# A gated mix of a long state-space convolution and a top-2 expert on one core: the hand-ordered kernel rewritten as one list-scheduled graph

## Chip, cores, metric

One core of one Trainium2 chip. The metric is the device time of one execution in microseconds (us), lower is better; the time before is the median of three runs.

## The reference, cut to what matters

```python
x = A_u                                            # 1 x 2048 x 512, bf16
g = sigmoid((x * gate_w).sum(-1))                  # one gate a token
# a: per channel d a kernel K[d, l] of 2048 lags from 128 complex modes n
dt = exp(log_dt); P = exp((dt * A)[:, :, None] * l)         # l in bf16
K  = einsum("dn,dnl,dn->dl", C, P, dt * B).real
a  = irfft(rfft(pad(x)) * rfft(pad(K)))[:2048] + x * Dskip  # along the tokens
# b: the two tokens with the largest r = x @ w_r go through an expert
y  = (silu(x_sel @ w_gate) * (x_sel @ w_up)) @ w_down * sigmoid(r_sel)
b  = x + scatter_add(0, idx, y)
out = g * a + (1 - g) * b
```

Rounding lags to bf16 leaves 2048 lags with few distinct values. Each distinct value is written as a sum of a lag t1 (table T1) and a lag t2 (table T2), so a tap is a product of two table rows summed over the 128 modes.

## The kernel before, in words

Everything runs on 128 partitions in bf16, with fp32 sums in PSUM. Helper functions record the operations: every vector tensor_tensor has line 306 (`TT`), tensor_scalar lines 309 and 310 (`TS`), copies 314 (`CP`), and every activation line 316 (`ACTV`). `Sched` (lines 46 to 117) keeps each engine's operations in the order in which the program names them and puts a wait in front of an operation for each buffer that it reads or writes, its own engine's last writer of that buffer included (lines 66 to 72). The order of the whole program is thus the order of the source, written by hand at lines 851 to 880.

- **Loads** (320 to 338): six parameter matrices, log_dt, the input u, gate vectors, expert matrices W_gate and W_up, and one 5.4 MB block of transform matrices, all issued at the start on SP's queue.
- **Parameters** (340 to 381): transposes on PE, then some twenty vector operations of 128x512 fp32.
- **Tables** (`lag_group`, 395 to 444, driven by `kgen_tables`, 629 to 658): for each half of 256 channels 32 lags of T1 and 21 of T2 in groups of four. Each lag has an exponential of its own (416), two phase arguments as int32 (403 on ScalarE or 406 on VectorE), and each group one sine over the low 16 bits; then products of magnitude and cosine or sine on VectorE, for T2 eight products and sums a group, since the weights C·B·dt are multiplied in.
- **Routing and expert** (`routing_and_moe`, 454 to 624): a generator of which one or two steps run between the table groups of the first half.
- **Taps** (`kgen_mm`, 659 to 678): per half 256 pairs of matmuls of 32x24 outputs, one pair a channel, with `tile_position`; 16-byte and 512-byte steps in their operands. 1024 matmuls in all stand at lines 670 and 674. `post` (679 to 714) gathers the taps of a chunk of 128 channels (690) and turns them into spectra of four blocks of 512 lags (707).
- **Convolution** by overlapped blocks of 512 for four chunks of 128 channels: `forward` (726, matmuls at 739), `products` (747, VectorE), `xu_inv` (770: (1-g)·x plus the expert row at 778 and 779, the inverse at 789, each evicted to SBUF by itself), and `mix_a`, `mix_p`, `mix_o` (830 to 842: skip term, gate, sum, store). The last chunk is done in four pieces (`final_fine`, 796).

Of the kernel before, what the change touches and what calls it, by code (L numbers as in the profile page):

```python
# [26 lines left out]

class Buf:

    def __init__(self, name, parents=()):  # L30
        self.name = name
        self.last_w = None
        self.readers = []
        self.parents = list(parents)

    def prior(self):
        out = []
        for p in self.parents:
            if p.last_w is not None:
                out.append(p.last_w)  # L40
            out.extend(p.readers)
            out.extend(p.prior())
        return out


class Sched:
    def __init__(self, nc, block_sems):
        self.nc = nc
        self.ops = {e: [] for e in ENGS}
        self.sem = dict(block_sems)  # L50
        self.cnt = {e: 0 for e in ENGS}
        self.known = {e: {} for e in ENGS}
        self.dma_sems = []
        self.dma_free = []
        self.final_waits = []

    def _deps(self, eng, reads, writes):
        deps = {}
        def add(ev):
            if ev is None:  # L60
                return
            s, v = ev
            k = id(s)
            if self.known[eng].get(k, 0) >= v:
                return
            if k not in deps or deps[k][1] < v:
                deps[k] = (s, v)
        for b in reads:
            add(b.last_w)
        for b in writes:  # L70
            add(b.last_w)
            for r in b.readers:
                add(r)
            for r in b.prior():
                add(r)
        out = list(deps.values())
        for s, v in out:
            self.known[eng][id(s)] = v
        return out

    def _commit(self, ev, reads, writes):
        for b in reads:
            b.readers.append(ev)
        for b in writes:
            b.last_w = ev
            b.readers = []

    def op(self, eng, fn, reads=(), writes=()):
        waits = self._deps(eng, reads, writes)
# [4 lines left out]
        return ev

    def dma(self, fn, sem, n=1, reads=(), writes=(), eng=SP, final=False):
        waits = self._deps(eng, reads, writes)
        ev = (sem, 16 * n)
        self.ops[eng].append((fn, waits, (sem, 16)))
        self._commit(ev, reads, writes)  # L100
        if final:
            self.final_waits.append(ev)
        return ev

    def emit(self, eng, h):
        for fn, waits, inc in self.ops[eng]:
# [54 lines left out]
def kspec_mats(L=2048):
    lq = bf16_lag(np.arange(L))
    rep = {}
    for j, t2 in enumerate(LQ_T2):
        for k, t1 in enumerate(LQ_T1):
            q = t1 + t2
            if q not in rep:
                rep[q] = (j, k)  # L170
    th = theta()
    out = np.zeros((len(KUSE), 128, 2 * BLK))
    cover = np.zeros(L, dtype=bool)
    for u, (i, jg) in enumerate(KUSE):
# [750 lines left out]
```

## Time and profile before

| what | value |
|---|---|
| runs | 374.71, 376.3, 377.43 us; median 376.3 |
| span of the profiled execution | 373.4 us (its first to its last instruction) |
| the same execution's own time | not listed apart from the three runs, which lie 1.3 to 4.0 us above the span |
| VectorE (DVE) busy | 270.7 us, 72% |
| ScalarE (ACT) busy | 239.4 us, 64% |
| TensorE (PE) busy | 188.9 us, 51%; mean granted clock 0.696 of full |
| HBM read, written | 14.27 MB, 2.10 MB |

Busy is the time in which an engine works on an instruction. Each row of an instruction view names line, engine, operation, output and input with their shapes, the count, busy time in us and the mean ns of one, and behind the last bar the idle time in front with what ended it. In the view of one source line the three numbers are the shortest, median and longest duration in ns, and then come the first and the last start. RT, RK, RS, RU and RC are the five SBUF arenas, ps is PSUM.

### The profile page before, as it was taken

The numbers are of one execution on the slowest core, as the hardware profiler recorded it, in microseconds if no ns is written. First come the engines' busy times: TensorE is split into PE (matmuls) and PEld (weight loads), VectorE is DVE, ScalarE is ACT, GpSimd is POOL, SyncE is SP. The second block draws the span as 40 slices with busy tenths as digits, with TensorE's granted clock in tenths as the row PEclk, the third lists the DMA queues.
The fourth block names the chain that finished last, engine by engine and source line by source line (L and its number), as shares of the span: only waits on it lengthen the run. The fifth ranks groups of instructions, "written<-read, shape, count | busy, mean of one in ns | idle before, by whom it ended". The sixth has DMA issues, their size and how long they took to land.

```text
span 373.4 us, 8503 instructions
## 1 busy us (share of the span) xinstructions
PE 188.9 (51%) x3674; PEld 170.3 (46%) x3674; DVE 270.7 (72%) x495; ACT 239.4 (64%) x385; POOL 1.7 (0%) x6
## 2 busy tenths in 40 slices
PE   2600301432300076704343803889899999998810
PEld 2500300330100076704343703789889889886810
DVE  0795658562599992878105999999999299899555
ACT  2899453399596999566999981553753484481461
POOL 0000010000000000000000000000000000000000
PEclk9855555555655556855856865689989969969785
DMA  6999000005000000000000000000000000200222
GB/s 154 275 443 438 26 3 0 0 11 187 0 1 0 0 4 5 2 1 2 1 2 0 2 0 2 4 4 4 2 2 2 3 2 2 58 3 2 58 67 45
DMA packets 18261, 16.91 MB, mean 45 GB/s; under 512 B 12848, under 2 KB 17072, under 8 KB 18096
## 3 DMA queue, kind: packets, MB, share of 16 engines
q1 hardware_dynamic: 18224, 16.37, 13.3%
q8 instruction: 29, 0.48, 0.5%
q14 instruction: 8, 0.07, 0.1%
HBM read 14.27 MB, written 2.10 MB: 44 GB/s over the span
## 4 chain that ended last, share of the span: by engine, by line
ACT 36%; DVE 32%; PE 26%; issue 4%; DMA 1%; SPq 1%; ACTq 0%; DVEq 0%
DVE RT L306 23%; ACT RT L316 21%; PE ps L739 10%; ACT RK L316 8%; PE ps L789 5%; DVE RT L310 5%; ACT L316 3%; PE ps L707 2%; ACT RT L837 2%; PE ps L670 2%; PE ps L674 1%; PE ps L779 1%; PE ps L778 1%; PE ps L607 1%; DVE RT L309 1%
## 5 line engine op out<-in xcount | busy, mean ns | idle before, releaser
L306 DVE TENSOR_TENSOR RT<-RT 128x1024 bf16<-128x1024 bf16 (+5 forms) x146 | 101.2, 704 | 29.7 <-ACT RT L316 19.3
L316 ACT ACTIVATE RT<-ps 128x512 bf16<-128x512 f32 (+3 forms) x79 | 51.8, 662 | 55.4 <-PE ps L739 22.8
L739 PE MATMUL ps<-RU,RC 128*128 128x128 bf16 x896 | 55.7, 228 | 16.7 <-ACT RK L316 16.6
L310 DVE TENSOR_SCALAR RT<-RS 128x256 int32<-128x256 f32 x148 | 49.2, 341 | 19.1 <-ACT RT L403 14.9
L739 PEld LDWEIGHTS ps<-RU,RC 128*128 128x128 bf16 x896 | 54.8, 103 | 17.1 <-issue 16.9
L306 DVE TENSOR_TENSOR RT<-RT,RK 128x4096 bf16<-128x4096 bf16 (+3 forms) x32 | 55.0, 1761 | 8.5 <-ACT RT L316 8.4
L316 ACT ACTIVATE RT<-RT 128x2048 bf16<-128x2048 int16 (+1 forms) x28 | 50.3, 1811 | 9.8 <-DVE RT L310 9.8
L670 PE MATMUL ps<-RT 128*32 128x24 bf16 x512 | 22.7, 286 | 52.1 <-DVE RT L306 52.1
L670 PEld LDWEIGHTS ps<-RT 128*32 128x32 bf16 x512 | 21.2, 171 | 52.9 <-DVE RT L306 52.4
L316 ACT ACTIVATE RT<-RS 128x256 bf16<-128x256 f32 x74 | 30.8, 416 | 3.5 <-DVE RS L306 1.2
L707 PE MATMUL ps<-RS,RC 128*128 128x128 bf16 x288 | 20.4, 240 | 20.2 <-ACT RS L316 17.6
L707 PEld LDWEIGHTS ps<-RS,RC 128*128 128x128 bf16 x288 | 19.5, 110 | 21.0 <-ACT RS L316 18.2
L316 ACT ACTIVATE RK<-ps 128x512 bf16<-128x512 f32 x32 | 19.1, 595 | 15.3 <-PE ps L707 5.9
L306 DVE TENSOR_TENSOR RT<-RT,RS 128x1024 bf16<-128x1024 bf16 (+1 forms) x48 | 27.8, 619 | 0.4
L789 PE MATMUL ps<-RT,RC 128*128 128x128 bf16 x384 | 27.7, 247 | 0.0
L403 ACT ACTIVATE RT<-RS 128x256 int32<-128x256 f32 x64 | 26.4, 416 | 1.9
L789 PEld LDWEIGHTS ps<-RT,RC 128*128 128x128 bf16 x384 | 27.2, 113 | 0.3
L837 ACT ACTIVATE RT<-RT,RS 128x128 bf16<-128x128 bf16 x48 | 19.2, 401 | 12.5 <-DVE RT L306 11.0
L674 PE MATMUL ps<-RT 128*32 128x24 bf16 x512 | 22.9, 286 | 3.8 <-issue 3.8
L674 PEld LDWEIGHTS ps<-RT 128*32 128x32 bf16 x512 | 21.8, 169 | 4.1 <-issue 4.1
L306 DVE TENSOR_TENSOR RT<-RK,RT 128x1024 bf16<-128x1024 bf16 x16 | 11.1, 691 | 13.2 <-ACT RT L316 12.9
L316 ACT ACTIVATE RK<-RS 128x256 bf16<-128x256 f32 x32 | 19.4, 605 | 1.0
(66 smaller groups left out, 189.8 us busy)
## 6 DMA issues: line engine op xcount, KB each, us to landing
RC<-c_mats SPq DMA_DIRECT2D x1, 5376.0 KB, 24.5
RU<-in_A_u_dram SPq DMA_DIRECT2D x4, 512.0 KB, 8.0
RK<-in_B_w_gate_dram SPq DMA_DIRECT2D x1, 1792.0 KB, 9.4
RK<-in_B_w_up_dram SPq DMA_DIRECT2D x1, 1792.0 KB, 13.4
RK<-in_B_w_down_dram SPq DMA_DIRECT2D x1, 1792.0 KB, 7.5
out_dram<-RT SPq DMA_DIRECT2D x3, 512.0 KB, 3.8
out_dram<-RT SPq DMA_DIRECT2D x4, 128.0 KB, 2.0
RT<-in_A_A_re_dram SPq DMA_DIRECT2D x1, 128.0 KB, 2.6
```

The source lines that it names most:

```text
L306: return S.op(eng, lambda h: h.tensor_tensor(out=o, in0=a_, in1=b_, op=op), reads=rd, writes=wr)
L309: return S.op(eng, lambda h: h.tensor_scalar(out=o, in0=a_, scalar1=s1, scalar2=None, op0=op0), reads=rd, writes=wr)
L310: return S.op(eng, lambda h: h.tensor_scalar(out=o, in0=a_, scalar1=s1, scalar2=s2, op0=op0, op1=op1), reads=rd, writes=wr)
L316: return S.op(ACT, lambda h: h.activation(out=o, in_=a_, func=func, scale=scale), reads=rd, writes=wr)
L403: S.op(ACT, lambda h, i=i, t=t, cs=cs: h.activation(out=ARG(0, 128, ((gi * 2 + cs) * 4 + i) * HC, (1, HC)), in_=B16(0, 128, c0, (1, HC)), ...
L607: last = h.matmul(P32(by_, 0, 2, 0, (1, D)), HB(0, 128, 6 * 28 + fb * 2, (1, 2)), WD(0, 128, fb * D, (1, D)), start=(fb == 0), stop=(fb == ...
L670: h.matmul(P32(b, 32 * c4, 32, cq * 24, (1, 24)), TP(0, 128, (ch // 8) * 512 + (ch % 8), (8, 32)), TQ(0, 128, ch, (HC, 24)), start=True, s ...
L674: last = h.matmul(P32(b, 32 * c4, 32, cq * 24, (1, 24)), TP(0, 128, (ch // 8) * 512 + 256 + (ch % 8), (8, 32)), TQ(0, 128, NSLOT * HC + ch ...
L707: last = h.matmul(P32(bb[hb_], 0, 128, tl * 128, (1, 128)), CM(0, 128, OF_KP + u * 1024 + tau * 128, (1, 128)), KC(0, 128, kb * 768 + KUSE ...
L739: last = h.matmul(P32(bb[hb_], 0, 128, tl * 128, (1, 128)), CM(0, 128, of + tc * 1024 + tau * 128, (1, 128)), U(0, 128, tb * D + ck * 128, ...
L789: last = h.matmul(P32(b, 0, 128, tt * 128, (1, 128)), CM(0, 128, OF_G + sc * 512 + tt * 128, (1, 128)), YHs[vb](0, 128, j * 1024 + sc * 12 ...
L837: S.op(ACT, lambda h, tb=tb, vb=vb: h.activation(out=YA(0, 128, vb * 2048 + tb * 128, (1, 128)), in_=YA(0, 128, vb * 2048 + tb * 128, (1, ...
```

## The change

A new class `Graph` takes every operation with the engines that may run it and a duration for each, a rank from a table of names, and its buffers. `schedule` walks through a simulated time: a free engine takes the ready operation of the highest rank for which SBUF and PSUM have room, and then SBUF addresses are packed. `link` puts in waits, leaving out those that an earlier wait already implies, and PE's waits for itself. The order of each engine is thus fixed before the program runs.

```diff
+RANKS = [("ld pnA", 990), ... ("exp z", 800), ("polar0", 790), ("exp t1_0", 640), ("sin0", 650),
+ ("X0", 646), ("X1", 635), ("A1_0", 600), ..., ("tap 0", 590), ("Kh 0", 580), ("sin1", 515), ("A1_1", 500),
+ ("spread", 495), ("tap 1", 490), ("Kh 1", 480), ("gather", 470), ("ffn", 470), ("Y0.0", 420), ("inv 0", 400),
+ ("ld inv", 400), ("ld w", 390), ("Y1.0", 320), ("inv 1", 300), ...]
+for o in avail[e]:                                  # schedule(): the choice of a free engine
+    if o.ready > t or (best is not None and o.prio <= best.prio): continue
+    if o.pref and e != o.pref and free[o.pref] < t + o.opts[e][1]: continue
```

The tables. Eight lags of T2 and its steps are made from exponential and sine (`DIRECT`), for 512 channels at once; the other lags are complex products of table rows (`cmul`, four products and two sums, four lags of 256 channels each), and the weights come in with the first product, for half h A1, A2, B, C, D:

```diff
+DIRECT = [129, 130, 131, 132, 4, 256, 512, 1024]
+for i, t in enumerate(DIRECT):
+    e1.append(g.op("exp z%d" % t, {ACT: (... ca(512))}, ...))
...
+    for cs in range(2):
+        g.op("arg z%d.%d" % (t, cs), {DVE: (... cd(512))}, [br], [ba[cs]])
+    for hh_ in range(2):
+        s1.append(g.op("sin z%d.%d" % (t, hh_), {ACT: (... ca(512))}, ba, [bZ[hh_][i]], after=e1))
+for hh_ in range(2):
+    for i0, n in ((0, 4), (4, 1), (5, 3)):
+        g.op("polar%d z%d" % (hh_, i0), {DVE: (pol, cd(512 * n))}, ...)
...
+for i, (pa, pb) in enumerate(((0, 0), (1, 1), (0, 1), (1, 0))):
+    g.op("%s.m%d" % (name, i), {DVE: (... op=ALU.mult), cd(n))}, ...)
+for part in range(2):
+    g.op("%s.a%d" % (name, part), {DVE: (... op=(ALU.subtract if part == 0 else ALU.add)), cd(n))}, ...)
```

(The last four lines are in `cmul`; n is 1024.) T1 has the lags 8·m for m from -16 to 15 (`T1K`). Sine and cosine are made for m = 1 to 16 and serve both signs; the products at the end are of 128x2048, two of them in each half of 128x1792:

```diff
+for m in [m for mm in range(1, 17) for m in (mm, -mm) if m != 16]:
+    e2.append(g.op("exp t1_%d %d" % (h, m), {ACT: (... out=tT1[h](BF, 0, 128, s * 4, (128, NG), (1, 4)), ... ca(256))}, ...))
...
+for q in range(8):
+    for cs in range(2):
+        for i in range(2):
+            g.op("arg%d %d.%d" % (h, m, cs), {DVE: (... cd(256)), ACT: (... ca(256))}, [br], [ba[2 * cs + i]], pref=DVE)
+    for cs in range(2):
+        sins.append(g.op("sin%d %d.%d" % (h, q, cs), {ACT: (... ca(512))}, ..., after=e2))
...
+for ck in range(2):
+    tt("t1_%d t1i+.%d" % (h, ck), ...); tt("t1_%d t1r+.%d" % (h, ck), ...)
+    g.op("neg sin %d.%d" % (h, ck), {DVE: ..., ACT: ...}, [], sq + [bsn[ck]], pref=DVE)
+    tt("t1_%d t1i-.%d" % (h, ck), ...); tt("t1_%d t1r-.%d" % (h, ck), ...)
```

The sines wait for all exponentials of their half (`after=e2`), and the exponentials of half 1 for the sines of half 0 (`after=after_e`). The forward transform is one of 1024 tokens for two blocks, 512 channels wide, folded by even and odd tokens; the taps take four channels a matmul:

```diff
+for j in range(eo, 8, 2):
+    r = h.matmul(o, tF(BF, 0, 128, ((j * 2 + ri) * 4 + ft) * 128, (1, 128)), tU(BF, 0, 128, (b * 8 + j) * D, (1, D)), ...)
+if b == 1:
+    r = h.matmul(o, ident() if plus else nident(), eov(0, 1 - ri, row, (1, D)), start=False, stop=True)
...
+tt("spread %d.%d.%d" % (b, ri, sd), ..., cd(2048))
...
+hh.matmul(o, tT1[h](BF, 0, 128, gr * 128, (1, 128)), tT2[h](BF, 0, 128, 4 * gr, (HC, NSL), (1, 4)), start=True, stop=False)
+r = hh.matmul(o, tTI[h](BF, 0, 128, gr * 128, (1, 128)), tT2[h](BF, 0, 128, NSL * HC + 4 * gr, (HC, NSL), (1, 4)), ...)
+TAP1 = g.ops[-1:]
...
+g.dma("ld wg", ..., 1835e3, writes=[bWG], after=TAP1, bias=-30)
+g.dma("ld wu", ..., 1835e3, writes=[bWU], after=TAP1, bias=-30)
+g.dma("ld inv%d" % b, ..., 1048e3, writes=[bG[b]], after=TAP1, bias=-10)
+g.dma("ld wd", ..., 1835e3, writes=[bWD], after=TAP1, bias=-30)
+g.dma("ld U2_%d" % b, ..., 1048e3, writes=[bU2[b]], after=TAP1)
```

That makes 32 rows of X with 4 matmuls (block 0) or 5 (block 1) of 512 columns, 8 `spread`, 64 groups of two tap matmuls of 84 columns a half, then a half 88 small matmuls `sel` and 104 `Kh` of 256 columns; what PE writes is evicted 1024 elements at a time. TAP1 is the last tap of half 1. W_down goes into W_gate's tile (`tWD = tWG`), so its load also waits for the first expert matmuls.

The spectra of K stay in SBUF as whole tiles of a half. The products are 40 operations of 128x2048 and 8 folds; the inverse adds (1-g)/g times x, the expert row and the convolution in PSUM, and the gate is the scale of its eviction, two of 128x256 for each of 16 `inv` (the skip term is the tap of lag 0: Dskip is a row of the spectrum's operand, `ld dskip`):

```diff
+o = ps(F32, 0, 128, (2 * hb + jj) * 256, (1, 256))
+hh.matmul(o, tDG(...), tU2[blk](...), start=True, stop=False)
+hh.matmul(o, tOR(BF, 0, 2, ...), tZB(BF, 0, 2, 1024 + h * HC, (1, HC)), start=False, stop=False)
+for ft in range(4):
+    for ri in range(2):
+        r = hh.matmul(o, tG(...), tS(...), start=False, stop=(ft == 3 and ri == 1))
...
+g.op("inv %d.%d.%d" % (h, blk, 2 * q + hb), {PE: (iv_, 0.109 * 20)}, bS + [bG[q], bDG, bOR[blk], bZB[2], bU2[blk]], ...)
+r = hh.activation(..., in_=ps(F32, 0, 128, i * 256, (1, 256)), func=ACTF.Copy, scale=g32(0, 128, blk * 8 + 4 * q + i, (1, 1)))
...
-        def xu_inv(ck): ...
-        def mix_a(ck): ...
-        def mix_p(ck): ...
-        def mix_o(ck): ...
```

## Rows read from the trace of the kernel before

**Rows 1.** Page, part 1: busy us, share of the span and instructions of each engine.
```profile
PE 188.9 (51%) x3674; PEld 170.3 (46%) x3674; DVE 270.7 (72%) x495; ACT 239.4 (64%) x385; POOL 1.7 (0%) x6
```

**Rows 2.** Page, part 4: the chain that ended last, shares by engine.
```profile
ACT 36%; DVE 32%; PE 26%; issue 4%; DMA 1%; SPq 1%; ACTq 0%; DVEq 0%
```

**Rows 3.** Stretches of the span: length, busy time by engine, PE clock, DMA.
```profile
52.00:101.00 49.00, 14.04 (x226) 9.11 (x226) 28.14 (x94) 29.98 (x46) 0.00 (x0) 0.53 0.11 38
...
357.00:374.00 17.00, 0.00 (x0) 0.00 (x0) 9.83 (x26) 5.10 (x10) 0.00 (x0) 0.63 0.27 62
...
250.00:326.00 76.00, 74.72 (x1187) 68.67 (x1184) 65.77 (x82) 39.34 (x75) 0.00 (x0) 0.93 0.04 9
```

**Rows 4.** Groups of DVE instructions by form.
```profile
L310 DVE TENSOR_SCALAR RT<-RS 128x256 int32<-128x256 f32 x148 | 49.2, 341 | 19.1 <-ACT RT L403 14.9
...
L306 DVE TENSOR_TENSOR RT<-RT 128x2048 bf16<-128x2048 bf16 x14 | 17.1, 1224 | 7.6 <-ACT RT L837 7.0
...
L306 DVE TENSOR_TENSOR RT<-RT 128x512 f32<-128x512 f32 x12 | 7.8, 687 | 0.2
...
L309 DVE TENSOR_SCALAR RT<-RT,RS 128x2048 bf16<-128x2048 bf16 x4 | 2.8, 748 | 4.7 <-ACT RT L316 4.7
```

**Rows 5.** DVE's instructions in order of time, merged: start us, us to the last's end.
```profile
11.34 0.43 DVE L314 CAST RT<-RS 128x512 f32<-128x512 bf16 x1 [11.34 <-ACT RS L316]
...
24.30 5.09 DVE L310 TENSOR_SCALAR RT<-RS 128x256 int32<-128x256 f32 x16
...
131.47 11.25 DVE L310 TENSOR_SCALAR RT<-RS 128x256 int32<-128x256 f32 x16
...
230.30 13.24 DVE L306 TENSOR_TENSOR RT<-RT,RK 128x4096 bf16<-128x4096 bf16 x2
...
280.00 2.35 DVE L306 TENSOR_TENSOR RT<-RT,RK 128x2048 bf16<-128x2048 bf16 x2
282.26 2.87 DVE L306 TENSOR_TENSOR RT<-RT 128x1024 bf16<-128x1024 bf16 x4
285.05 1.29 DVE L306 TENSOR_TENSOR RT<-RT,RK 128x1024 bf16<-128x1024 bf16 x2
...
324.75 4.49 DVE L306 TENSOR_TENSOR RT<-RT,RK 128x4096 bf16<-128x4096 bf16 x2 [1.62 <-ACT RT L316]
```

**Rows 6.** Groups of ACT instructions by form.
```profile
L316 ACT ACT_TABLE_LOAD x12 | 15.4, 1283 | 0.9 <-PEq L910 0.7
...
L316 ACT ACTIVATE RT<-ps 128x1024 bf16<-128x1024 bf16 x8 | 8.2, 1022 | 0.6
...
L316 ACT ACTIVATE RT<-RT 128x512 bf16<-128x512 int16 x2 | 1.2, 612 | 0.0
```

**Rows 7.** ACT's instructions in order of time, merged.
```profile
12.53 14.31 ACT L316 ACTIVATE RT<-RS 128x256 bf16<-128x256 f32 x32 [1.22 <-DVE RS L306]
...
190.92 1.27 ACT L316 ACTIVATE RK<-ps 128x512 bf16<-128x512 f32 x2
192.08 5.19 ACT L403 ACTIVATE RT<-RS 128x256 int32<-128x256 f32 x12
```

**Rows 8.** PE: line 739 in a stretch; lines 586 and 670 by source.
```profile
249.35:261.87 12.52, 12.51 (x224) 12.33 (x221) 1.00 0.01 3
...
L586 PE MATMUL ps<-RS,RK x112: 163/165/165, 80.9 to 83.8; 128*128 128x2 bf16 x112
...
L670 PE MATMUL ps<-RT x512: 218/286/377, 131.6 to 243.2; 128*32 128x24 bf16 x171
```

**Rows 9.** Page, parts 2 and 6: GB/s in 40 slices; DMA issues with us to landing.
```profile
GB/s 154 275 443 438 26 3 0 0 11 187 0 1 0 0 4 5 2 1 2 1 2 0 2 0 2 4 4 4 2 2 2 3 2 2 58 3 2 58 67 45
...
RK<-in_B_w_down_dram SPq DMA_DIRECT2D x1, 1792.0 KB, 7.5
...
out_dram<-RT SPq DMA_DIRECT2D x4, 128.0 KB, 2.0
RT<-in_A_A_re_dram SPq DMA_DIRECT2D x1, 128.0 KB, 2.6
```

More of the change, by code (lines that the diff above doesn't have):

```diff
@@ L1 @@
+import heapq
 import math
@@ L28, with __init__ @@
 class Buf:
-    def __init__(self, name, parents=()):
-        self.name = name
-        self.last_w = None
+    def __init__(self, tile):
+        self.tile = tile
+        self.last_w = []
         self.readers = []
[L34 to L47, printed above, removed]
-        self.nc = nc
[L49 to L67, printed above, removed]
+class Op:
+    __slots__ = ("name", "opts", "preds", "succs", "tiles", "prio", "npred", "ready", "eng", "start",
+                 "fin", "idx", "mem", "dma", "bytes", "final", "num", "i", "pref", "clock")
@@ L68, in _deps @@
         for b in reads:
-            add(b.last_w)
+            for w in b.last_w:
+                o.preds[w.i] = w
         for b in writes:
-            add(b.last_w)
+            for w in b.last_w:
+                o.preds[w.i] = w
             for r in b.readers:
[L73 to L81, printed above, removed]
+                o.preds[r.i] = r
@@ L96, in dma @@
[L96 to L106, printed above, removed]
+        ts = {}
+        for b in list(reads) + list(writes):
+            if b.tile is not None:
+                ts[id(b.tile)] = b.tile
@@ L163, in kspec_mats @@
[L163 to L182 removed]
+T1K = [s if s < 16 else -(s - 15) for s in range(32)]
@@ L183, in kspec_mats @@
                 ls = np.nonzero(lq == q)[0]
-                ls = ls[(ls >= BLK * i) & (ls < BLK * (i + 1))]
+                ls = ls[ls >= 1024] - 1024 if u == 4 else ls[ls < 1024]
                 if len(ls) == 0:
                     continue
-                cover[ls] = True
-                t = ls - BLK * i
-                out[u, 32 * g + k, :BLK] = np.cos(np.outer(t, th)).sum(0)
-                out[u, 32 * g + k, BLK:] = -np.sin(np.outer(t, th)).sum(0)
-    assert cover.all(), "some lags are not covered by KUSE"
@@ L192, in kspec_mats @@
[L192 to L208 removed]
+                cover[ls + (1024 if u == 4 else 0)] += 1
@@ L211, in bass_gated_mix__ssm_conv_s4__moe_arch_mod__prompt_kernel @@
+                out[u, 32 * qd + s] = spec(ls)
+    misc0[0] = 1.0
+    misc0[64] = 1.0
+    cover[0] += 1
+    s1024 = T1K.index(15)
+    assert base[MISC[1]] + 8 * 15 == 1024
+    ls = np.nonzero(lq == 1024)[0]
+    ls = ls[ls >= 1024]
+    out[5, 32 + s1024] = spec(ls - 1024)
+    cover[ls] += 1
+    assert (cover == 1).all(), "lags are not each covered once"
+    return out, misc0
+DIRECT = [129, 130, 131, 132, 4, 256, 512, 1024]
 def bass_gated_mix__ssm_conv_s4__moe_arch_mod__prompt_kernel(nc, A_u, A_A_re, A_A_im, A_B_re, A_B_im, A_C_re, A_C_im, A_log_dt, A_Dskip,
```

1593 lines of the change are left out of this document (906 added, 687 removed), and 11 rows, old and new, of the table RANKS.

## Prediction

> **What bounds the kernel now.** Begin with the busy times [rows 1]: DVE works 270.7 us of 373.4, ACT 239.4, PE 188.9, so no engine is full. The chain of waits says the same [rows 2]: ACT 36%, DVE 32%, PE 26% of it, so the end is set by engines that hand over to each other. Dividing the three busy times by the span, (270.7 + 239.4 + 188.9) / 373.4 = 1.87 engines work at a time. The stretches show where this is worse [rows 3]: from 52 to 101 us, where the first half's tables, the routing and the expert are mixed by hand, (14.0 + 28.1 + 30.0) / 49 = 1.47, and in the last 17 us PE is idle while one chunk is added, gated and stored in four steps. At its best, from 250 to 326 us, DVE is busy 65.8 of 76 us, 87%. So two things can make it shorter: less work on DVE and ACT, and less waiting.
>
> Rows 5 and 7 show a price that the writing of the old kernel adds. Where an instruction writes the buffer of the one before, it waits for it: four sums of 128x1024 in a row take 2.87 us, 0.72 each. Where it doesn't, the next starts earlier: of two products the second ends 1.29 us after the first began, so it started 0.60 after. For 128x2048 the pair takes 2.35 [rows 5] against 1.224 for one [rows 4], a start every 1.13; in a chain 1.24. ACT does the same: 32 exponentials of 128x256 into one buffer take 14.31 us, 0.447 each, but an instruction with another target starts at 192.08, when the one before ends at 190.92 + 1.27 = 192.19, so 0.11 earlier [rows 7].
>
> **DVE after the change, counted.** The new graph has finer buffers, so I price by a mix of both starts.
> - Parameters: 12 operations of 128x512 fp32 at 0.69 [rows 4]: 8.3 us.
> - Arguments of the eight direct lags: 16 of 128x512. The old ones of 128x256 take 5.09 / 16 = 0.32 each in one buffer [rows 5]; less the 0.12 that 1024 gains by free starts that is 0.20. Estimate for twice the size 0.40: 6.4 us.
> - Polar products: 8192 elements in all, at 1.18 per 2048: 4.7 us.
> - Chained products: 10 `cmul` of 6 operations, four free at 0.60 and two chained at 0.72, 0.64 on average: 38.4 us.
> - T1: 64 arguments at 0.20, 12.8 us (0.32 would make 20.4); 16 products at 1.18 and 4 sign changes at 0.75 [rows 4]: 21.9 us.
> - Routing and expert steps, about 45 small ones and the diagonal: 10 us, an estimate with ends 5 and 20, since ACT may take some.
>
> That is D1 = 102.5 us up to the last table product. After it come 8 `spread` (9.4 us, which may also fill gaps before) and 48 products and folds at 1.18, 56.6 us. DVE's sum is 168.5 instead of 270.7.
>
> **ACT and PE.** ACT: 62 exponentials at 0.31 to 0.447; 48 sines and 8 exponentials of 128x512 at 0.50 to 0.61; some 52 evictions of 1024 at 0.91 to 1.02; 7 table loads at 1.28 [rows 6]; 32 gated evictions of 256, about 0.4 by the slope between 612 ns at 512 and 1022 at 1024. With the lower prices 19 + 28 + 47 + 9 + 13 + 6 (rest) = 122 us, of which some 93 belong to the table phase; with the upper ones about 108 there. Both are under the 118 us that DVE needs below, so ACT runs close behind and not in front. PE: 224 matmuls of 128 columns take 12.51 us at a granted clock of 1.00 [rows 8], 0.437 ns a column. [...]
>
> **The path to the end, step by step.**
> 1. Start: DVE's first instruction was at 11.34 [rows 5], after all six parameter loads and log_dt. Now it needs the first pair (2.6 us to landing [rows 9]), its transposes and one exponential. I take 7; ends 5 and 11.3.
> 2. Tables: 102.5 us at the best overlap seen, 87% [rows 3], because DVE waits for ACT's sines and for table loads: 117.8, so 124.8.
> 3. Contention while taps run. Two products of 128x4096 take 4.49 us at 324.75 and 13.24 at 230.30, when the strided tap matmuls of lines 670 and 674 run [rows 8]; 16 arguments take 5.09 at 24.30 and 11.25 at 131.47, under the taps of the other half [rows 5]. That is 6.2 to 8.8 us lost a half in 13 us. The new taps are four times fewer, their weights are contiguous, and their columns are still picked with steps of 512 bytes. Their 128 a half take 128 x 84 x 0.437 = 4.7 us, 9.4 at the lower clock, so 0 to 6 us a half; I put 3 on the path, for half 0: 128. [...]
> 4. Taps of half 1, 7 us: 135. They release the loads that the change moves here from the start: inverse matrices, u a second time, W_gate and W_up, 7.7 MB, in 17.4 us at the 443 GB/s of the fullest slice, and 2 to land [rows 9]: 154.5. Until then SP's queue holds nothing that could have gone earlier; behind these loads come only W_down and the stores. At the start their cover was complete, here nothing covers them for PE's inverse.
> 5. Expert: 112 matmuls took 80.9 to 83.9 [rows 8], half of that before W_down may be overwritten onto W_gate's tile: 156. W_down 7.5 us [rows 9]: 163.6. Its 14 matmuls of 512 columns, 3.1 to 6.3 us: 168.6. Three small steps on two rows, 2 us: 170.6.
> 6. All 16 inverses wait for that, since the expert row is added in their PSUM: a wait that the old inverse (line 789), whose sum stood alone, did not have. Behind it in PE's queue stand only other inverses. 320 x 256 x 0.437 = 35.8 us (71.6 at 1.2 GHz): 206.4. Last gated eviction 0.7 and store 2.0 [rows 9]: 209.
>
> Beside it runs DVE: from 128, `spread` to 137, and products and folds, back to back as at 280 to 286 us [rows 5], to 194; the spectra of half 1 come at 135 + 3 (`sel`) + 11.6 (`Kh`) + 2, about 152, before half 0's products end at 166, so no gap. Then the last four inverses 9 us, eviction and store: 206. The two ends lie 3 us apart, so the stall of one is covered by the other, and neither alone is worth shortening by more than that. What goes without a successor is the old tail: sums, gate and extra evictions of the last 17 us [rows 3].
>
> The span is then 209 us. The old span is 373.4 in a run whose own time is not given; the median of the runs is 376.3, 2.9 more, and I add these: **212 us**.
>
> **The rivals.**
> - *Hand-overs cost nothing.* The list keeps DVE full in the tables and the taps disturb nobody: 15.3 + 3 less, 194 us. For it: long stretches of DVE at full pace in rows 5. Against it: seven table loads and sines that wait for 31 exponentials.
> - *The old overlap stays.* [...] For it: the order is fixed from estimated durations, and each error is a wait at the head of a queue. Against it: three engines have independent work until 135.
> - *Short runs cost double.* T1 is written in runs of 4 elements, 8 bytes; the old T1 in runs of 8 elements took the normal 0.447 [rows 7], shorter ones no row shows. If each such ACT instruction doubles, 62 x 0.31 + 32 x 0.50 = 35 us come onto ACT, 93 becomes 128, 10 to 28 more than DVE's pace allows: 222 to 240 us. [...]
> - *The fixed order inverts, and it is slower than before.* The place is the table phase: an operation listed early stands at the head of ACT's or DVE's queue and waits for one that stands behind another waiting head, so engines take turns. [...]
>
> **How the numbers follow.** Chances: forecast (200 to 226) 0.57, free hand-overs (185 to 200) 0.18, old overlap (226 to 262) 0.17, short runs 0.05, inverted order 0.03. The range goes from 188 to 250: it takes in the inverses at the lower clock throughout (248), and the bounds of start, small steps and arguments, and leaves out the top of the old overlap and the lowest free case. One per cent, about 4 us, is what a measurement of this kernel can tell from no change. All cases but the last end far below: faster 0.96, within 1% 0.01, slower 0.03.
>
> **What would show it.** DVE busy near 168 us and ACT near 122; the chain passing from DVE's tables through the taps to the loads of W_gate and W_up and on to line after line of inverse matmuls; PE idle between half 1's spectra and the expert's last row. Wrong are: step 2 if DVE's last T1 product lies far from 125 us; step 4 if the expert's matrices land long before the spectra are done with; step 6 if inverses start as DVE's folds end and not after the expert; step 3 if DVE's products keep 1.2 us each while taps run.

## The result, and the profile after

The changed kernel takes 214.2 us (median of 4 runs, 210.1 to 218.6) where the kernel before took 375.5 on the same chip: a ratio of 0.560 with an interval of [0.556, 0.564]. The ratio, here and below, is over undisturbed runs alone (210.1 and 211.2 us, at a mean granted clock of 0.874 and 0.868; the other two, at 217.1 and 218.6, had 0.856 and 0.849). The forecast was 212.0. The profiled execution took 211.2 us, its span is 209.4; the forecast had 209 for the span. The sum is right, but four of its terms are not: they cancel, and that they do is luck.

The page of the changed kernel, parts 1 and 4 (busy time and share of the span; the chain that ended last, by engine), against [rows 1, 2]. In the views of the changed kernel RB is SBUF and RP is PSUM:

```profile
PE 145.9 (70%) x1479; PEld 99.1 (47%) x1482; DVE 155.0 (74%) x249; ACT 136.0 (65%) x260; POOL 2.1 (1%) x10
...
PE 42%; ACT 38%; DVE 13%; DMA 3%; issue 2%; ACTq 1%
```

DVE gave up 115.7 us, ACT 103.4, PE 43. The engines fill 65 to 74% of the span each, now (145.9 + 155.0 + 136.0) / 209.4 = 2.09 of them at a time against 1.87. DVE's share of the chain fell from 32% to 13%: PE and ACT have 80% of it. Where each of them holds it is seen in the stretches of the changed kernel (stretch, length, busy us and instructions of PE, weight loads, DVE, ACT and POOL, then PE clock, DMA share, GB/s), against [rows 3]:

```profile
8.00:60.00 52.00, 38.02 (x166) 16.77 (x170) 46.31 (x102) 48.77 (x90) 0.94 (x3) 0.93 0.20 76
60.00:77.00 17.00, 11.45 (x227) 10.69 (x228) 17.00 (x21) 14.09 (x21) 0.00 (x0) 0.80 0.54 202
77.00:117.00 40.00, 18.28 (x227) 14.51 (x220) 36.60 (x68) 37.13 (x83) 0.94 (x3) 0.74 0.01 1
117.00:125.00 8.00, 8.00 (x156) 7.59 (x157) 5.56 (x18) 6.14 (x12) 0.00 (x0) 0.82 0.68 257
125.00:146.00 21.00, 19.51 (x381) 17.73 (x377) 20.97 (x18) 12.16 (x19) 0.00 (x0) 1.00 0.76 288
146.00:161.00 15.00, 4.89 (x14) 1.46 (x14) 15.00 (x17) 2.34 (x5) 0.00 (x0) 0.65 0.33 111
161.00:206.00 45.00, 44.72 (x320) 29.59 (x320) 13.40 (x12) 12.78 (x32) 0.00 (x0) 0.93 0.14 42
...
170.00:180.00 10.00, 10.00 (x79) 6.78 (x76) 4.40 (x4) 2.96 (x8) 0.00 (x0) 1.00 0.19 54
```

Up to 117 us the tables run, ACT busy 93% and DVE 92% of the time from 77 on. From 117 to 146 come the taps and spectra of half 1. Then PE works 4.9 us of 15, and after 161 it does the 320 matmuls of the inverse and nothing else: DVE works only 13.4 us there. The DVE timeline (start, us to the end of the last of the merged instructions, count, idle time before) shows the stations, against [rows 5]. Line 617 is the helper for products and sums:

```profile
7.82 0.69 DVE L600 SCALAR_TENSOR_TENSOR RB<-RP,RB 128x512 f32<-128x512 bf16 x1 [7.82 <-PE RP L584]
...
68.88 9.16 DVE L617 TENSOR_TENSOR RB<-RB 128x2048 bf16<-128x2048 bf16 x8
...
91.62 1.23 DVE L617 TENSOR_TENSOR RB<-RB 128x2048 bf16<-128x2048 bf16 x1 [1.03 <-ACT RB L901]
...
96.38 3.49 DVE L617 TENSOR_TENSOR RB<-RB 128x2048 bf16<-128x2048 bf16 x3
...
117.30 2.35 DVE L617 TENSOR_TENSOR RB<-RB 128x2048 bf16<-128x2048 bf16 x2
...
144.33 5.76 DVE L617 TENSOR_TENSOR RB<-RB 128x2048 bf16<-128x2048 bf16 x5
...
153.67 0.17 DVE L1061 TENSOR_TENSOR RB<-RB 128x28 bf16<-128x28 bf16 x1
```

The eight `spread` came at 68.88, between the tables of the two halves, and beside half 0's taps (68.7 to 75.7). The four at 91.62 and 96.38 are products of half 0's spectra, which thus begin among the tables of half 1. The expert's small steps (line 1061 is the last) stand between products of 128x2048. ACT's timeline of the changed kernel, against [rows 7]:

```profile
9.51 1.02 ACT L612 ACTIVATE RB<-RP 128x1024 bf16<-128x1024 bf16 x1 [3.76 <-PE RP L584]
10.43 4.26 ACT L638 ACTIVATE RB<-RB 128x512 bf16<-128x512 f32 x8
...
28.07 1.28 ACT L721 ACT_TABLE_LOAD   x1
...
36.37 6.24 ACT L721 ACTIVATE RB<-RB 128x256 bf16<-128x256 f32 x20
...
112.90 0.63 ACT L738 ACTIVATE RB<-RB 128x512 bf16<-128x512 int16 x1 [0.33 <-DVE RB L732]
```

One exponential starts every 0.31 us (6.24 / 20): each writes a buffer of its own, and the wait of [rows 7] with its 0.447 is gone. The copy of the third pair of parameters (line 612) stands in front of the eight exponentials and waits 3.76 us. And the end, on PE's timeline:

```profile
142.28 3.00 PE L1050 MATMUL RP<-RB 128*128 128x2 bf16 x112
153.98 4.89 PE L1066 MATMUL RP<-RB 128*2 128x512 bf16 x14 [8.70 <-DVE RB L1061]
161.06 0.40 PE L1136 MATMUL RP<-RB 128*128 128x256 bf16 x1 [2.19 <-ACT RB L955]
```

### The profile page after: what moved, and what is told of

It is laid out like the page before. It is cut to its first block, busy times and chain, and to the rows that moved or that the text cites. A ratio compares the mean times of both kernels' runs of the same rounds, so it can differ in the third digit from the quotient of the medians.

```text
span 209.4 us, 3594 instructions
## 1 busy us (share of the span) xinstructions
PE 145.9 (70%) x1479; PEld 99.1 (47%) x1482; DVE 155.0 (74%) x249; ACT 136.0 (65%) x260; POOL 2.1 (1%) x10
## 4 chain that ended last, share of the span: by engine, by line
PE 42%; ACT 38%; DVE 13%; DMA 3%; issue 2%; ACTq 1%
PE RP L1140 16%; DVE RB L617 9%; ACT RB L721 8%; PE RP L896 7%; ACT RB L738 6%; ACT RB L796 5%; ACT RB L901 4%; PE RP L1137 3%; ACT RB L928 3%; DMA RB<-in_A_B_im_dram 3%; PE RP L838 3%; PE RP L839 2%; PE RP L1066 2%; ACT RB L638 2%; PE RP L1136 2%
## 5 line engine op out<-in xcount | busy, mean ns | idle before, releaser
L617 DVE TENSOR_TENSOR RB<-RB 128x2048 bf16<-128x2048 bf16 (+3 forms) x76 | 85.7, 1182 | 3.4 <-PE RP L839 1.8
L789 PE MATMUL RP<-RB 128*128 128x512 bf16 x125 | 34.4, 416 | 13.5 <-ACT RB L796 7.3
L1140 PE MATMUL RP<-RB 128*128 128x256 bf16 x256 | 35.8, 286 | 0.0
L1148 ACT ACTIVATE RB<-RP,RB 128x256 bf16<-128x256 f32 x32 | 13.4, 471 | 32.2 <-PE RP L1140 32.2
L789 PEld LDWEIGHTS RP<-RB 128*128 128x128 bf16 x128 | 12.9, 105 | 32.4 <-ACT RB L796 9.0
L896 PE MATMUL RP<-RB 128*128 128x256 bf16 x208 | 24.9, 283 | 4.4 <-ACT RB L874 3.6
L1140 PEld LDWEIGHTS RP<-RB 128*128 128x128 bf16 x256 | 23.4, 102 | 7.2 <-issue 0.7
L668 DVE TENSOR_TENSOR RB<-RB 128x1024 bf16<-128x1024 bf16 x40 | 25.2, 682 | 0.1
L896 PEld LDWEIGHTS RP<-RB 128*128 128x128 bf16 x208 | 20.7, 101 | 8.7 <-ACT RB L874 4.2
L721 ACT ACTIVATE RB<-RB 128x256 bf16<-128x256 f32 x62 | 20.3, 413 | 0.0
L901 ACT ACTIVATE RB<-RP 128x1024 bf16<-128x1024 f32 x16 | 15.8, 1030 | 6.5 <-PE RP L896 6.5
L738 ACT ACTIVATE RB<-RB 128x512 bf16<-128x512 int16 x32 | 17.6, 616 | 0.3 <-DVE RB L732 0.3
L796 ACT ACTIVATE RB<-RP 128x1024 bf16<-128x1024 f32 x16 | 15.5, 1012 | 1.6 <-PE RP L792 1.6
L838 PE MATMUL RP<-RB 128*128 128x84 bf16 x128 | 13.3, 224 | 4.0 <-DVE RB L617 2.6
L838 PEld LDWEIGHTS RP<-RB 128*128 128x128 bf16 x128 | 12.6, 114 | 4.7 <-DVE RB L617 2.9
L839 PE MATMUL RP<-RB 128*128 128x84 bf16 x128 | 13.3, 223 | 0.0
L671 DVE TENSOR_TENSOR RB<-RB 128x1024 bf16<-128x1024 bf16 x20 | 12.9, 682 | 0.0
L839 PEld LDWEIGHTS RP<-RB 128*128 128x128 bf16 x128 | 12.6, 113 | 0.1
L1136 PE MATMUL RP<-RB 128*128 128x256 bf16 x32 | 9.1, 286 | 2.2 <-ACT RB L955 2.2
```

The lines of the kernel that those rows point to most:

```text
L617: return g.op(name, {DVE: (lambda h: h.tensor_tensor(out=o(), in0=a(), in1=b(), op=op), cost)}, rd, wr, bias=bias, **kw)
L668: g.op("%s.m%d" % (name, i), {DVE: (lambda h, i=i, pa=pa, pb=pb: h.tensor_tensor(out=tv(i, inp_a[1]), in0=inp_a[0](pa), in1=inp_b(pb), op= ...
L721: e2.append(g.op("exp t1_%d %d" % (h, m), {ACT: (lambda hh, m=m, s=s, h=h: hh.activation(out=tT1[h](BF, 0, 128, s * 4, (128, NG), (1, 4)), ...
L738: sins.append(g.op("sin%d %d.%d" % (h, q, cs), {ACT: (lambda hh, ta=ta, cs=cs, tt_=tt_, q=q: hh.activation(out=tt_(BF, 0, 128, 8 * q, (4, ...
L789: r = h.matmul(o, tF(BF, 0, 128, ((j * 2 + ri) * 4 + ft) * 128, (1, 128)), tU(BF, 0, 128, (b * 8 + j) * D, (1, D)), start=(j == eo), stop= ...
L796: g.op("ev X%d.%d.%d" % (b, ri, pr), {ACT: (lambda h, ps=ps, b=b, pr=pr, ri=ri: h.activation(out=eov(b, ri, 2 * pr, (1, 1024)), in_=ps(F32 ...
```

## The experiments

Times are medians; each ratio is to the kernel before on the same chip (375.5 to 377.5 us in these comparisons), and each span is that of one profiled run.

**The expert's row.** Is the wait of all 16 inverses for the row what PE loses at the end?

```
e1:  -  hh.matmul(o, tOR(BF, 0, 2, ...), tZB(BF, 0, 2, ...), start=False, stop=False)
     -  bS + [bG[q], bDG, bOR[blk], bZB[2], bU2[blk]]
     +  bS + [bG[q], bDG, bU2[blk]]
e2:  -  ("ld w", 390)
     +  ("ld wg", 410), ("ld wu", 409), ("ld wd", 408)
```

> Leaves out the expert row in the inverse's PSUM and with it the wait of all 16 inverses for the expert (the two chosen tokens lack the expert's part). Theory A (the wait for the expert sets the start of the tail, and PE's 45 us of inverses end it): the first inverse starts at about 143 us, when the spectra of half 1 are done, instead of 161; the end is then set by DVE's last fold at about 174 plus four inverses (9 us) and a store: span about 186 instead of 209. Rival B (DVE's folds set the start of most inverses anyway): the first inverses start earlier, the last end stays within 5 us of 209 less the time of the 32 row matmuls.

e1 took 193.7 us, ratio 0.508 [0.504, 0.512], span 190.8: its first inverse started at 147.95 instead of 161.06 and its last ended near 187; the last four inverses came after DVE's last fold (177.4). That is Theory A. Near 143 and 186 were expected; but the taps of half 1 started 3.0 us later than in the changed kernel (120.0), and the expert's 112 matmuls stood in front of the inverses until 148. The wait and the 32 row matmuls together are worth 209.4 - 190.8 = 18.6 us of span, and more, since line 612 came 3.6 us later in e1's run (13.09). A part of it is the clock: PE was granted 1.00 from 140 to 188 in e1, and 0.51 during the first thirty inverse matmuls of the changed kernel.

> Only ranks: W_gate, W_up and W_down come ahead of the inverse matrices in the list. Theory A (the expert's row is late because its matrices are queued behind 4 MB of others): W_up lands about 9 us earlier, the row is ready at about 150 instead of 160, and the span falls by 5 to 10 us, as long as the inverse matrices still land before 150. Rival B (W_down, which waits for the first expert matmuls, and DVE's queue ahead of the small expert steps set the row): less than 3 us.

e2 took 214.1 us, ratio 0.568 [0.565, 0.571]: no gain (Rival B). PE's timeline of e2 shows what happened:

```profile
138.99 1.60 PE L1050 MATMUL RP<-RB 128*128 128x2 bf16 x56 [3.00 <-DMA RB<-in_B_w_gate_dram]
140.44 12.84 PE L896 MATMUL RP<-RB 128*128 128x256 bf16 x104
153.12 1.54 PE L1050 MATMUL RP<-RB 128*128 128x2 bf16 x56
```

With another rank the list was made anew, and it put the second half of the expert's matmuls behind the 104 spectrum matmuls, and the product of line 1061 behind seven products on DVE (it came at 157.83). The matrices were asked for first, yet the first inverse came at 166.17, 5.1 us later, of which 4.4 are a later start of the tables. So it is not the loads alone that make the row late: it is the place of the expert's steps in the queues of PE and DVE.

**What the row matmul itself costs.** Within the inverse ten matmuls took 1.30 us where 10 x 256 columns at [rows 8]'s pace are 1.12. The weight loads of the changed kernel show where the rest goes (timeline of PEld):

```profile
184.70 0.10 PEld L1136 LDWEIGHTS RP<-RB 128*128 128x128 bf16 x1
185.01 0.09 PEld L1137 LDWEIGHTS RP<-RB 2*128 2x128 bf16 x1 [0.21 <-issue]
185.22 0.77 PEld L1140 LDWEIGHTS RP<-RB 128*128 128x128 bf16 x8
```

Of ten loads one stands apart: 0.21 us idle before the load of two rows. e3 gives the row matmul 128 rows, 126 of them zeros set by POOL:

```
-  hh.matmul(o, tOR(BF, 0, 2, ...), tZB(BF, 0, 2, ...), ...)
+  hh.matmul(o, tOR(BF, 0, 128, ...), tZB(BF, 0, 128, ...), ...)
```

> The expert row's matmul gets 128 rows of weights and data, 126 of them zero, instead of 2; everything else stays. In the trace of the changed kernel ten matmuls of an inverse take 1.30 us, and the weight loads of the two-row matmul and of the one behind it start 0.21 us after the one before, not ahead. Theory A (a change of the number of rows keeps the next weights from being loaded ahead, twice 0.1 us for each of 32): ten take 1.09 us and the span falls by 6 to 7 us. Rival B (ten matmuls of 256 columns simply cost 1.30 us, 0.51 ns a column): no change within 1 us.

e3 took 205.3 us (202.4 to 207.3), ratio 0.539 (202.9 / 376.7), span 200.6 in the profiled run. The same stretch of e3 as above:

```profile
170.00:180.00 10.00, 10.00 (x94) 8.95 (x93) 5.33 (x5) 3.83 (x10) 0.00 (x0) 1.00 0.18 53
```

94 matmuls instead of 79 in 10 us at the same clock: 0.106 us each against 0.127 (Theory A). No weight load of e3 stands apart: they start at 184.68, 184.79 and 184.90. Here 126 more rows of zeros were cheaper than two rows alone. But the span fell by 8.8 us where 32 x 0.21 are 6.7. About 3 more go with the granted clock at the beginning of the inverses, 0.50 against 1.00. The changed kernel:

```profile
162.00:165.00 3.00, 3.00 (x15) 1.74 (x14) 3.00 (x3) 0.00 (x0) 0.00 (x0) 0.50 0.00 0
```

and e3:

```profile
162.00:165.00 3.00, 3.00 (x29) 2.69 (x28) 3.00 (x4) 0.75 (x2) 0.00 (x0) 1.00 0.00 0
```

PE had been idle for 8.70 us in front of the expert's last matmuls there, and for 7.08 in e3; what sets the granted clock is not shown.

**Who sets the end of the tables?** The prediction said DVE. e5 puts known work on ACT, e6 takes known work from DVE; the fixed order stays in both.

```
e5:  +  if m < -4:
     +      g.op("exp t1_%d %d again" % (h, m), {ACT: (..., 0.0)}, [bal], [bT1e[h][s]], ...)
e6:  -  ev(m0, npl), ev(m0, npl), cvw(npl), ALU.mult
     +  ev(m0, 1), ev(m0, 1), cvw(1), ALU.mult
```

> 24 of the 62 exponentials of the lag table are computed a second time into the same place, by an instruction of its own on ACT; the list's durations and so the order of everything else stay. Nothing else is changed. That adds 24 x 0.31 to 0.45 = 7.4 to 10.7 us to ACT and nothing to DVE. Theory A (the tables are bound by ACT, which the windows show busy nearly without a gap from 10 to 69 us and from 77 to 114): the last table product comes 7 to 11 us later than at 116.9, near 126, and the run takes 7 to 11 us more than after, about 219 to 224. Theory B (DVE sets the end of the tables, as the prediction had it): ACT has room, the last table product stays within 2 us of 117 and the time within 2 us of after. Theory C (the two share the bound, neither alone): 3 to 6 us later.

> The eight products that multiply the real part of the lag table by its cosines are cut to one lag of 7 or 8 each (so that the real part of the others is left without its cosine); the order of everything stays. That takes 8 x (1.14 - about 0.2) = 7 to 8 us from DVE before the taps and nothing from ACT. Theory A (ACT sets the end of the tables): only the very last product, which stands behind the last sines, comes earlier by its own 1 us, the tables end at 115 to 117, and the time falls by 0 to 2 us. Theory B (DVE sets it): the tables end near 109 to 110 and the time falls by 7 to 8 us, to about 206. Theory C (shared): 3 to 5 us earlier.

e5 took 229.0 us, ratio 0.606 [0.603, 0.610]; e6 213.0, ratio 0.561 [0.556, 0.565]. ACT's timeline of e5 (line 724 holds the repeated exponentials, and the sines moved from line 738 to 741):

```profile
32.80 1.28 ACT L721 ACT_TABLE_LOAD   x1
...
47.22 3.47 ACT L724 ACTIVATE RB<-RB 128x256 bf16<-128x256 f32 x11
...
58.24 1.28 ACT L724 ACT_TABLE_LOAD   x1
59.54 0.42 ACT L724 ACTIVATE RB<-RB 128x256 bf16<-128x256 f32 x1
...
66.44 1.28 ACT L741 ACT_TABLE_LOAD   x1
...
130.66 0.63 ACT L741 ACTIVATE RB<-RB 128x512 bf16<-128x512 int16 x1 [0.39 <-DVE RB L735]
```

and of e6:

```profile
31.12 1.28 ACT L721 ACT_TABLE_LOAD   x1
...
115.99 0.63 ACT L738 ACTIVATE RB<-RB 128x512 bf16<-128x512 int16 x1 [0.38 <-DVE RB L732]
```

The chain from the first table load of line 721 to the last sine is 112.90 - 28.07 = 84.8 us in the changed kernel, 84.9 in e6 and 97.9 in e5. e5's addition came out larger than planned, since in each half one repeated exponential fell between the sines and brought two table loads: 2 x (3.4 + 1.28 + 0.42 + 1.28) = 12.8 us of ACT, of which 13.0 came through. Some 7 us less on DVE moved nothing. In this order ACT sets the end of the tables (Theory A). Of the 227.5 - 209.4 = 18.1 us of span another 4.7 are the start: 32.80 instead of 28.07, because the third pair's second load took 10.0 us to land instead of 6.2, and line 612 held ACT back for 7.08 us instead of 3.76.

**The old contention.** Under the new taps DVE kept its pace: 9.16 us for eight products (1.14 each), 2.35 for two, as in [rows 5] without taps. Which property of the old taps had slowed it? e4 gives half 0 the old kind of steps in the weights, half 1 in the data; b1 and b2 take the steps out of the kernel before.

```
e4:  half 0:  tT1[h](BF, 0, 128, gr * 112, (8, 128))        half 1:  tT2[h](BF, 0, 128, gr, (HC, NSL), (64, 4))
b1:  -  TP(0, 128, (ch // 8) * 512 + (ch % 8), (8, 32))     +  TP(0, 128, (ch // 8) * 512 + (ch % 8) * 32, (1, 32))
b2:  -  TQ(0, 128, ch, (HC, 24))                            +  TQ(0, 128, ch * 24, (1, 24))
```

> Taps read other elements than they should (the taps are wrong): half 0 takes its weights in steps of 16 bytes, as the kernel before did, half 1 its data in single elements of 2 bytes in steps of 128 and 512 bytes instead of runs of 8 bytes. Number and size of the matmuls stay. Theory A (strided weights slowed DVE under the old taps): DVE's products of 128x2048 start every 1.14 us under half 1's taps and take 2 us or more under half 0's. Theory B (strided data did): the other way round. Theory C (neither; it was the many matmuls of 32 columns at tile positions): 1.14 under both.

e4 took 222.8 us, a single run. DVE's timeline and, below, the stretch of half 1's taps:

```profile
68.81 9.17 DVE L617 TENSOR_TENSOR RB<-RB 128x2048 bf16<-128x2048 bf16 x8
...
117.09 2.35 DVE L617 TENSOR_TENSOR RB<-RB 128x2048 bf16<-128x2048 bf16 x2
```

```profile
117.00:137.50 20.50, 20.50 (x146) 17.45 (x145) 5.46 (x15) 7.52 (x12) 0.00 (x0) 0.50 0.28 103
```

That is Theory C: DVE is not touched by either (9.17 us for eight products, 2.35 for two), so neither step alone slowed it under these matmuls of 84 columns. The single elements cost PE itself time: about 21 us for the taps of half 1 (116.8 to 137.7, granted clock 0.50) instead of 7.8 (granted clock 0.82). By the 0.437 ns of the forecast 128 x 84 columns would take 9.4 us at a clock of 0.50, an estimate.

> The kernel before, with the tap matmuls of lines 670 and 674 reading their 32 weight columns side by side instead of 16 bytes apart (other weights, so other taps); their data stay picked with steps of 512 bytes, and everything else stays. It asks which operand made DVE and ACT slow under the old taps. Theory A (the weights' steps): 16 arguments under the taps take 5 to 6 us instead of 11.25, the two products of 128x4096 about 4.5 instead of 13.24, 32 exponentials about 14.3 instead of 20.35. Theory B (the data's steps): all three stay at 11.3, 13.2 and 20.4. Theory C (neither alone, or only the rate at which the matmuls come): they stay as they were here and in the run with contiguous data too.

> The kernel before, with the tap matmuls of lines 670 and 674 reading their 24 data columns side by side instead of 512 bytes apart (other data, so other taps); their weights stay 16 bytes apart. Theory A (the weights' steps slow DVE and ACT): 11.25, 13.24 and 20.35 us stay. Theory B (the data's steps): 5 to 6 us for the arguments, about 4.5 for the two products, about 14.3 for the exponentials. Theory C: as they were.

One run each: b1 374.3 us, b2 372.7; the kernel before 376.5. The line of ACT under the taps of the kernel before, which [rows 7] does not show:

```profile
122.72 20.35 ACT L316 ACTIVATE RK<-RS 128x256 bf16<-128x256 f32 x32
```

The timelines of DVE and ACT, first b1:

```profile
123.70 18.99 ACT L316 ACTIVATE RK<-RS 128x256 bf16<-128x256 f32 x32
...
132.45 9.94 DVE L310 TENSOR_SCALAR RT<-RS 128x256 int32<-128x256 f32 x16
...
230.09 8.75 DVE L306 TENSOR_TENSOR RT<-RT,RK 128x4096 bf16<-128x4096 bf16 x2
```

then b2:

```profile
123.06 14.32 ACT L316 ACTIVATE RK<-RS 128x256 bf16<-128x256 f32 x32
...
131.81 5.09 DVE L310 TENSOR_SCALAR RT<-RS 128x256 int32<-128x256 f32 x16
...
229.20 4.48 DVE L306 TENSOR_TENSOR RT<-RT,RK 128x4096 bf16<-128x4096 bf16 x2
```

Theory B for the most part: with the data side by side all three are back at the undisturbed values of [rows 5, 7], to 0.01 us, though they still lie beside the taps (in b2 from 131.9 to 144.3 and from 229.3 to 241.5). With the weights side by side they lose a part of the slowness (13.24 to 8.75, 11.25 to 9.94). So the matmuls' data, picked 512 bytes apart, slowed DVE and ACT, and the steps of the weights made it worse. b2 against the kernel before shows it for DVE with 5.09 against 11.25 us; beside the taps of the changed kernel DVE lost nothing, 1.14 us a product. What in the new taps spares DVE stays open: they differ from the old ones in the width of the matmuls, in `tile_position` and in the runs of 4 elements, and e4's single elements have only 128 bytes between them.

**A version that beats both.** e7 takes e3 and adds the row of half 0 last: the accumulation is opened by one matmul of 512 columns with weights of zero, and the row is an operation of its own.

```
+  if h == 0: hh.matmul(ps(F32, 0, 128, hb * 512, (1, 512)), tZW(...), tU2[blk](...), start=True, stop=False)
-  bS + [bG[q], bDG, bOR[blk], bZB[2], bU2[blk]]
+  bS + [bG[q], bDG, bU2[blk]] + ([bZW] if h == 0 else [bOR[blk], bZB[2]])
+  if h == 0: g.op("inv %d.%d.%d row" % (...), {PE: (ir_, 0.109 * 2)}, [bOR[blk], bZB[2]], [bp], bias=bias)
```

> The version with the row matmul on 128 rows, and for half 0 the row is no longer inside the inverse: the accumulation of two time blocks is opened by one matmul of 512 columns with weights of zero (8 x 0.22 = 1.8 us more), diagonal and 16 spectral matmuls follow without the expert, and the row is added by an operation of its own which stands behind the expert and all 8 inverses of half 0 in PE's order. Half 1 is as it was. Theory A (only the wait for the row holds PE back): the first inverse starts near 148 instead of 161, three pairs of blocks run ahead of the expert's last matmuls, which no longer start from an idle PE, PE then works without a gap: 148 + 8 x 2.18 + 4.8 + 1.8 + 8 x 2.18 = 189.5, and the low clock and the last store make a span of 193 to 196 against 200.6 with the row on 128 rows alone; about 196 to 199 as a median. Theory B (PE gains nothing since DVE's folds or the order of PE's queue hold it in the place of the row): inverses start early but stand still later, the last ends as before near 196, and the span stays at 199 to 203.

e7 took 198.5 us, ratio 0.523 [0.520, 0.527], span 194.1: 0.523 / 0.560 = 0.935 of the changed kernel. PE's timeline of e7:

```profile
147.78 0.48 PE L1137 MATMUL RP<-RB 128*128 128x512 bf16 x1
...
156.08 3.18 PE L1067 MATMUL RP<-RB 128*2 128x512 bf16 x14
...
170.11 1.91 PE L1156 MATMUL RP<-RB 128*128 128x256 bf16 x16
```

The first inverse starts at 147.78, the expert's last matmuls (line 1067) follow a PE at work and take 3.18 us instead of 4.89, and the rows of half 0 come at 170.11, when nobody waits for them any more. Theory A, with both numbers inside its ranges.

**Can the tables be shortened too?** e8 puts line 612 behind the eight exponentials, e9 puts all 64 arguments on DVE, e10 takes e6's work from DVE in e8's order.

```
e8:  -  ("cp B", 700)        +  ("cp B", 830)
     -  bias=250)            +  bias=250, after=e1)
e9:  -  DVE: (...), ACT: (lambda ...: hh.activation(... func=ACTF.Copy ...), ca(256))}, ..., pref=DVE)
     +  DVE: (...)}, ...)
```

> The version with the late row, and the copy of the third pair of parameters (line 612), which stood at the head of ACT's queue in front of the eight exponentials of line 638 and waited 3.8 to 7.9 us there for a load whose landing differs from run to run, is put behind those exponentials; DVE's products with it move behind the arguments. The list is scheduled anew. Theory A (that wait is on the path, since ACT sets the end of the tables): the exponentials start at 9.2 to 9.5 us instead of 10.4 to 14.8, the last table product comes 2 to 6 us earlier than in the run with the late row, the span of the profiled run is 188 to 192 against 194.1, the median 193 to 196 against 198.5, and the runs lie closer together. Theory B (the copy only waits elsewhere, or the new order loses it again): no change beyond 1.5 us, 197 to 200.

> The run before this one, with all 64 arguments of the lag table on DVE; 15 of them stood on ACT between the sines and the evictions (line 735, 0.3 to 0.45 us each). ACT gives up about 5 us, DVE takes 15 x 0.2 to 0.3 = 3 to 4.5 us. Theory A (ACT alone sets the end of the tables, and DVE has room): 2 to 5 us less than the run before this one. Theory B (with the earlier start DVE is as late as ACT, so that the work only moves): within 1.5 us of it. Theory C (DVE, with products of the spectra behind the tables in its queue, becomes the bound): 2 to 5 us more.

> The run with the third pair behind the exponentials, in the same order, with the eight products by the cosines cut to one lag each as in the run with less work on DVE (the real part of the other lags is left without its cosine): 7 to 8 us less on DVE up to the taps. It asks why the earlier sines bought nothing there: the last sine came at 105.2 us instead of 114.3 (run with the late row), but the last table product still at 119 to 120. Theory A (in the new order DVE sets the end of the tables, since the chained products that used to fill its waits for sines now stand behind them): the last table product comes 3 to 7 us earlier, near 113 to 116, and the time falls by 3 to 7 us from 200.1, to 193 to 197. Theory B (the end of the tables is set elsewhere, by the routing's transposes in PE's queue or by space in SBUF): the taps start as before near 118 and the time stays within 1.5 us of 200.1, as it stayed in the first run with less work on DVE.

e8 took 200.1 us, 0.532 [0.531, 0.533]; e9 201.3, 0.534 [0.532, 0.536]; e10 198.2, 0.526 [0.524, 0.527]. By the ratio none beats e7's 0.523. e9 lies 1.2 us above e8, its Theory B: the work only moved. ACT's and PE's timeline of e8:

```profile
9.20 4.27 ACT L616 ACTIVATE RB<-RB 128x512 bf16<-128x512 f32 x8 [3.18 <-DVE RB L602]
...
104.56 0.64 ACT L738 ACTIVATE RB<-RB 128x512 bf16<-128x512 int16 x1
...
117.86 0.25 PE L838 MATMUL RP<-RB 128*128 128x84 bf16 x1 [2.04 <-DVE RB L671]
```

The exponentials start at 9.20 instead of 11.24 in e7, the last sine comes at 104.6 instead of 113.7, and the taps start at 117.9 where e7's started at 117.8. In the new order the chained products of half 1 (lines 668, 671) stand behind the table products on DVE, which then works without a gap from 102.9 to 117.8: ACT's earlier end is spent on DVE. e10 was to show that DVE is the bound there, and Theory A fell: with some 4 us less on DVE in half 1 the taps started at 118.76, since DVE now stood idle for ACT, 3.23 us at 99.30, and 1.38 for line 896. These products don't read its results, so the wait is taken to be for a place in SBUF that half 0's spectrum matmuls had not yet left:

```profile
99.30 1.09 DVE L624 TENSOR_TENSOR RB<-RB 128x1792 bf16<-128x1792 bf16 x1 [3.23 <-ACT RB L738]
...
110.06 1.29 DVE L668 TENSOR_TENSOR RB<-RB 128x1024 bf16<-128x1024 bf16 x2 [1.38 <-PE RP L896]
```

Three things then end the tables within a few us of each other: ACT's sines, DVE's products and the release by line 896. Where e10's 1.9 us against e8 come from, with the taps no earlier, stays open.

## Why the prediction was right, point by point

- *Start*, DVE at 7: 7.82. Right, but it was ACT's start that counted, and the head of ACT's queue (line 612) was not in the sum: 3.76 us here, up to 7.9 in other runs, by the landing of one load.
- *Tables*, step 2, "118 us that DVE needs", end at 124.8, ACT "close behind and not in front": wrong in the engine and 8 us too long. The last table product ended at 116.9. e5 and e6 show that ACT sets it. From 8 to 117 us ACT was busy 48.8 + 14.1 + 37.1 = 100.0 us, where the sum had some 93, or 108 by its upper prices. DVE was busy 46.3 + 17.0 + 36.6 = 99.9, 92% and not 87%; but the eight `spread` (9.1) and four products of half 0 (4.6) are in that. So the tables' own work on DVE was some 86 us and not 102.5: routing put 1.4 us in front of 117 instead of 10, 15 of the 64 arguments ran on ACT, and the other terms were up to 2 us too high. Over the whole span this shows as DVE 155.0 and ACT 136.0, where 168 and 122 were named as signs.
- *Contention*, step 3, 3 us: 0. The bound of 0 was in the range; the value was taken from the old taps without asking which of their properties did it. b1 and b2 give the answer for the old taps, the steps of the data; why the new ones, still 512 bytes apart, cost DVE nothing (1.14 us a product beside them) is not shown.
- *Taps and loads*, step 4: taps 7.8 us, to 124.7 (7 predicted), the matrices landed at 142.7, 18.0 us after the taps' end (19.5 predicted). Right in time, but not by the wait that was named. TAP1 is the last tap in the source only; it ran first (its 336 columns are evicted at 117.77), and u's second load, which waits for it too, was issued at 118.55. The others were issued at 124.96 to 127.0, as the taps ended; the order has them wait for the space that the tables of half 1 occupied.
- *Expert*, step 5, 16.1 us from the landing to the row: 18.3. The 2.2 us are those between W_down's landing at 151.8 and line 1066's start at 153.98, when line 1061 stood behind products in DVE's queue. The step had every instruction and no queue.
- *Inverse*, step 6, 35.8 us: 44.8 (161.0 to 205.8), the largest error in one term. 32 x (1.30 - 1.12) = 5.8 us are the row matmuls (e3), which the sum put at the price of any other, 1.12 for ten. About 3 are the lower clock at its beginning: the first thirty matmuls took 6.85 us (161.06 to 167.91, granted clock 0.51) and thirty later ones 3.90 (granted clock 1.00). No run shows the 1.2 GHz that step 6 names for its upper value of 71.6 us: the traces show a granted share of full speed, 0.50 in the kernel before from 128 to 144 us and here from 162 to 165, where the eight spectral matmuls of a block took 1.89 us against 1.05 at 1.00. That the inverses wait for the row is right: e1.
- *The second end*, DVE's folds at 194 and end 206: DVE's 48 products and folds took 55.4 us (56.6 predicted), four of them among the tables and the others from 117.3 to 174.4, 20 us earlier than the forecast. "The two ends lie 3 us apart" is wrong: without the row the end was at 190.8 (e1), so the row was worth 18.6 us alone, and e7 took 15.3 us (209.4 - 194.1) by moving and padding it.

Summed up: -7.9 (tables) - 3.2 (contention, rounding) + 0.8 - 1.5 (taps, loads) + 2.2 (expert) + 9.0 (inverse) + 1.0 (last eviction and store) = +0.4 us: 209.4 against 209. That -11.1 in the first two terms and +9.0 in the inverse nearly meet is luck. Of the rivals, the free hand-overs were right about the contention; in the tables the measured 116.9 lies between their 109.5 and the forecast's 124.8. The short runs were wrong outright: one exponential with runs of 8 bytes lasted 413 ns on the mean, and one of the old ones, outside the taps, 416.

## What to carry to other kernels

A term that is ready late belongs at the end of an accumulation and in an operation of its own; check when each input of the last long stage is ready before asking how long the stage is. In a list of fixed order, ask of each engine by putting known work on it: 12.8 us that came through as 13.0 found the bound that busy shares of 93% and 92% could not. And a shorter chain on one engine is worth only the distance to the next, so price that distance before the edit: e8 gained 9 us of sines and no time.

## What was not expected of the hardware

- In the changed kernel a matmul with weights of 2 rows between matmuls with weights of 128 rows cost 0.21 us more than one with 128 rows in e3 (ten took 1.30 us against 1.09); with 126 rows of zeros more, 94 matmuls ran in the time of 79.
- In the kernel before, the data of 24-column matmuls, picked 512 bytes apart, slowed other engines by a factor of 1.4 to 3.0 (14.32 to 20.35 us on ACT, 5.09 to 11.25 and 4.48 to 13.24 on DVE), and side by side, in b2, by nothing.
- One load of 128 KB took 6.2 us to land in the changed kernel, 10.0 in e5 and 10.4 in e2, which issue the same loads up to there, and with it the start of ACT's chain moved by 4 us (line 612 at 9.51, 13.45 and 13.86).
